# Cluster attention, then token mixing: argmax's equality in PSUM, masks on other engines, later mixing weights converted in the second half

## The chip, the cores and the metric

One core of a Trainium2 chip runs the kernel. The metric is the device time of one execution in microseconds; the median of several runs counts. The engines are TensorE (PE, with its weight loads PEld), VectorE (DVE), ScalarE (ACT), GpSimd (POOL) and SyncE (SP), whose queue issues most DMAs.

## The reference

For 4 batches and 8 heads of 768 tokens and width 64, each query and key is assigned to the nearest of 16 centroids, and a query sees only keys of its own cluster. The result, as rows of 512 channels, goes through a rotation by learned angles, a mixing over tokens with two 768 x 768 weights, and a channel mixing with a residual:

```python
q_assign = np.argmax(np.einsum('bhsd,hcd->bhsc', q_n, c_n), axis=-1)
k_assign = np.argmax(np.einsum('bhsd,hcd->bhsc', k_n, c_n), axis=-1)
mask = q_assign[:, :, :, None] == k_assign[:, :, None, :]
scores = np.where(mask, scale * np.matmul(q, k.transpose(0, 1, 3, 2)), -1000000000.0)
attn = np.exp(scores - np.max(scores, axis=-1, keepdims=True))
attn = attn / (np.sum(attn, axis=-1, keepdims=True) + 1e-09)
x = np.matmul(attn, v)            # as (batch, token, 512)
theta = x @ w_theta
y = np.einsum('ts,bsd->btd', w_tok_r, x * np.cos(theta))
y = y + np.einsum('ts,bsd->btd', w_tok_i, x * np.sin(theta))
u = x + y
return u + np.maximum(u @ w_ch, 0.0)
```

The weights w_theta, w_tok_r, w_tok_i and w_ch come as 64-bit floats. The kernel makes 32-bit floats of their bits itself, and splits every operand of its large products into a high and a low part.

## The kernel before, in words

**First half: attention.** The work goes by pairs of heads, 16 of them (4 per batch). Each pair has 12 units (two halves of the queries, six blocks of 128 keys). A loop takes two units at a time. In each turn PE makes score products for the current units (sc, line 374), score products for the maxima of units 10 ahead (m, also line 374), and the products of the exponentials with v (av, line 509). ScalarE takes the exponentials (line 437), VectorE the row maxima (nm, line 396), and GpSimd adds up exponentials (acc, line 448). Side work for later pairs is hung into the loop at fixed units by tables of numbers: A_UNITS for the assignment to clusters, W_UNITS and W_EVERY for the conversion of weights. Within the loop, each engine's instructions keep the order in which the code issues them; before and after it a scheduler orders them.

The assignment of a pair (assign, line 248) runs in steps. PE makes the logits of queries and keys against the centroids (lg) and transposes them into a tile of PSUM (lt). From the third pair on, lt takes its turn in a pool of two tiles (m_tile, line 196) with the score tiles of the maxima, so the second m tile after lt uses the same place. VectorE takes the maximum over the 16 centroids (mxl), compares (line 280), multiplies by falling weights so that the first of equal maxima wins (line 284), and takes the maximum (rr). The cluster numbers go through DRAM to 16 rows per head (clq, clk). From them come the two mask rows mq and mk, which add a huge negative number to a score product where the clusters differ (lines 330 to 340): mq by two ScalarE passes (for the second pair by GpSimd), mk by VectorE.

The row sums of a pair (sm, line 476) go through DRAM (sd), are turned to one over them on VectorE (sq, line 494), and come back (rb, line 499) for the normalisation (line 530).

**Weights.** to_f32 (line 118) loads a block of 64-bit weights, and makes 32-bit floats by one ScalarE pass (line 135) and four VectorE operations (lines 137, 140, 143, 146). split_w (line 150) makes the high part on ScalarE and the low part on GpSimd (line 159). During the attention half w_theta and the mixing weights of the first three token blocks are converted and kept in SBUF; those of the last three blocks (six pieces) are converted too and stored to DRAM as 32-bit floats (wd3r to wd5i, line 156).

**Second half: mixing.** For each batch and token block, theta (line 804) makes the angle product (tp, line 608), VectorE reduces the angle (kk, r, lines 613 to 615) and turns the block of x (xn, line 601), ScalarE takes sine and cosine, VectorE multiplies, and GpSimd makes the low parts (zlc, zls, line 830). mix (line 866) adds 48 products per block to y in PSUM. theta runs two blocks ahead of mix. After six blocks add_y (line 880) adds y to x on VectorE (line 887), and the channel products (line 899) follow. During the first batch, late (line 783) brings the remaining mixing weights from DRAM into u tiles (a ring of four), splits them on ScalarE and VectorE (lines 790 and 791), and converts w_ch in four chunks through the same ring; the channel's own operands use that ring next.

## Time and profile before

| | |
|---|---|
| median of 3 runs | 792.06 us (789.42 to 792.98) |
| the profiled execution | 792.87 us; its span 791.1 us |
| PE busy | 774.3 us |
| VectorE busy | 572.6 us |
| GpSimd busy | 488.3 us |
| ScalarE busy | 386.5 us |
| granted TensorE clock, mean | 0.991 |
| first product of the mixing | at 462.4 us |

How to read it: the profiled execution is one run, and its span reaches from the first to the last instruction. In rows of a timeline the first number is the start in us, the second the duration, then the engine and the line of the kernel, the operation, the tiles written and read, and in brackets how long the engine sat idle before it and what ended that. A busy PE is not PE at its peak.

### The profile page before, as it was taken

To read this page: it belongs to the slowest core of one execution; us is meant where nothing else is said; L and a number is where in the kernel's file an instruction comes from. 1 tells how busy PE (TensorE), PEld (TensorE's weight loads), DVE (VectorE), ACT (ScalarE), POOL (GpSimd) and SP (SyncE) were. 2 spreads that over 40 slices of the span, in tenths; PEclk is the share of its full clock that TensorE was granted. 3 is DMA by queue.
4 is the path that set the end of the run, shared out by engine and by line. 5 is a ranking of instruction groups with operands and counts; after the bars stand their busy time and mean duration, and the time that the engine had idled before them with its cause. 6 is when DMAs were issued, how large, how long until landed. Compare 5 with 4: busy or idle time off the path is not lost.

```text
span 791.1 us, 14306 instructions
## 1 busy us (share of the span) xinstructions
PE 774.3 (98%) x5538; PEld 572.9 (72%) x5538; DVE 572.6 (72%) x688; ACT 386.5 (49%) x777; POOL 488.3 (62%) x284
## 2 busy tenths in 40 slices
PE   6999999999999999999999799999999999999998
PEld 4656665666656565656665488899889988899998
DVE  5789999999999999999989659954445433634322
ACT  3366666767676676767556436341334123403310
POOL 3388789999999999888988432561215122332131
PEclk9899999999999999999999999999999999999999
DMA  3132324332433244324343467115011411030001
GB/s 120 61 98 72 93 95 151 93 123 91 151 104 125 81 149 151 119 84 164 112 161 109 101 182 206 24 31 173 15 27 28 160 27 27 14 94 15 1 21 61
DMA packets 81583, 73.43 MB, mean 93 GB/s; under 512 B 59588, under 2 KB 65324, under 8 KB 81132
## 3 DMA queue, kind: packets, MB, share of 16 engines
q1 hardware_dynamic: 81228, 72.10, 30.5%
q8 instruction: 43, 0.70, 0.4%
q10 hardware_dynamic: 288, 0.43, 0.1%
q14 instruction: 24, 0.20, 0.1%
HBM read 57.08 MB, written 15.32 MB: 92 GB/s over the span
## 4 chain that ended last, share of the span: by engine, by line
PE 91%; DVE 5%; DMA 2%; issue 1%; SPq 1%; ACT 1%; DVEq 0%
PE y L876 26%; PE sc L374 24%; PE av L509 15%; PE tp L608 8%; PE cy L899 5%; PE m L374 4%; PE cp L899 3%; PE sm L476 2%; PE lg L263 2%; PE y L899 1%; DVE acc L452 1%; PE lt L275 1%; DVE nm L396 1%; PE mt L404 1%; DVE xl L583 1%
## 5 line engine op out<-in xcount | busy, mean ns | idle before, releaser
L437 ACT ACTIVATE at<-sc 128x384 f32<-128x384 f32 x384 | 173.6, 493 | 96.0 <-PE m L374 50.5
L396 DVE TENSOR_REDUCE nm<-m 128x1 f32<-128x768 f32 x192 | 179.6, 945 | 21.4 <-PE m L374 18.3
L448 POOL TENSOR_TENSOR acc<-at,at 128x768 f32<-128x768 f32 x64 | 129.9, 2030 | 36.0 <-ACT at L437 36.0
L374 PE MATMUL m<-hk,hq 64*128 64x384 f32 x384 | 147.1, 387 | 0.9 <-DVE nm L396 0.8
L509 PE MATMUL av<-at,vt 128*64 128x384 f32 x768 | 145.7, 499 | 1.4 <-ACT at L437 1.2
L830 POOL TENSOR_TENSOR zlc<-ab,zhc 128x512 fp32r<-128x512 f32 x24 | 32.1, 1336 | 173.2 <-ACT zhc L828 173.2
L448 POOL TENSOR_TENSOR acc<-acc,at 128x768 f32<-128x768 f32 x64 | 132.4, 2068 | 10.1 <-ACT at L437 8.0
L374 PE MATMUL m<-mk,mq 64*128 64x384 f32 x384 | 127.7, 336 | 0.8 <-DVE mk L303 0.8
L374 PE MATMUL sc<-hq,hk 64*128 64x384 f32 x384 | 116.6, 388 | 0.5 <-ACT at L437 0.5
L374 PEld LDWEIGHTS sc<-hq,hk 64*128 64x128 f32 x384 | 55.8, 184 | 62.7 <-issue 27.9
L374 PE MATMUL sc<-mq,mk 64*128 64x384 f32 x384 | 97.6, 335 | 0.0
L374 PE MATMUL sc<-hq,lk 64*128 64x384 f32 x384 | 97.3, 334 | 0.0
L374 PE MATMUL sc<-lq,hk 64*128 64x384 f32 x384 | 97.3, 334 | 0.0
L509 PEld LDWEIGHTS av<-at,vt 128*64 128x64 f32 x768 | 46.7, 136 | 60.5 <-issue 53.6
L374 PEld LDWEIGHTS m<-hk,hq 64*128 64x128 f32 x384 | 70.7, 185 | 3.4 <-DVE nm L396 2.8
L374 PEld LDWEIGHTS m<-mk,mq 64*128 64x128 f32 x384 | 71.6, 188 | 1.1 <-ACT hq L356 1.1
L613 DVE TENSOR_SCALAR kk<-tp 128x512 int32<-128x512 f32 x24 | 16.4, 683 | 77.2 <-PE tp L608 77.2
L452 DVE TENSOR_TENSOR acc<-acc,acc 128x768 f32<-128x768 f32 x30 | 70.6, 2354 | 0.0
L581 ACT CAST xh<-xT 128x512 fp32r<-128x512 f32 x23 | 14.3, 622 | 99.7 <-PE tp L608 99.7
L890 POOL TENSOR_TENSOR ul<-xT,uh 128x384 fp32r<-128x384 f32 (+1 forms) x36 | 33.5, 957 | 35.4 <-ACT uh L889 34.9
L374 PEld LDWEIGHTS sc<-lq,hk 64*128 64x128 f32 x384 | 54.9, 186 | 0.0
L374 PEld LDWEIGHTS sc<-mq,mk 64*128 64x128 f32 x384 | 54.7, 184 | 0.0
(160 smaller groups left out, 1710.3 us busy)
## 6 DMA issues: line engine op xcount, KB each, us to landing
rawq<-in_qT_dram SPq DMA_DIRECT2D x16, 384.0 KB
vt<-in_v_dram SPq DMA_DIRECT2D x16, 384.0 KB
rb<-sd SPq DMA_DIRECT2D x32, 192.0 KB
xT_d<-xt SPq DMA_DIRECT2D x16, 384.0 KB
xb<-xT_d SPq DMA_DIRECT2D x96, 64.0 KB
rawk<-in_kT_dram SPq DMA_DIRECT2D x15, 384.0 KB
w<-in_wrT_dram SPq DMA_DIRECT2D x6, 768.0 KB
w<-in_wiT_dram SPq DMA_DIRECT2D x6, 768.0 KB
```

Source lines behind the costliest of these rows:

```text
L374: nc.tensor.matmul(out, lhsT=stat[r, cols], rhs=mov[r, over], start=start, stop=stop)
L396: nc.vector.tensor_reduce(out=s["nm", a][:, j, i // 2:i // 2 + 1], in_=s["m", j][:, :, 0:HS], op=ALU.max, axis=AX.XY, negate=True)
L437: last_exp[0] = nc.scalar.activation(out=s["at", a, i][:, j], in_=s["sc", j], func=AF.Exp, scale=SCALE)
L448: last_acc[0] = nc.gpsimd.tensor_tensor(out=s["acc", a, x], in0=prev, in1=at, op=ALU.add)
L452: nc.vector.tensor_tensor(out=s["acc", a, 0], in0=s["acc", a, 0], in1=s["acc", a, 1], op=ALU.add)
L509: nc.tensor.matmul(s["av"][64 * j:64 * j + 64], lhsT=s["vt"][:, i, j, :], rhs=s["at", a, i][:, j], start=(i == 0), stop=(i == NT - 1))
L608: nc.tensor.matmul(tp, lhsT=xx[:, c, :], rhs=w_th[c][k], start=(n == 0), stop=(n == 3 * NCT - 1))
L613: nc.vector.tensor_scalar_mul(kk, tp, INV_2PI)
L830: nc.gpsimd.tensor_tensor(out=zl, in0=tr, in1=zh.bitcast(F32), op=ALU.subtract)
L876: nc.tensor.matmul(y_at(b, d, c0, c1), lhsT=zz[:, d * P:(d + 1) * P], rhs=ww[:, c0:c1], start=first and lead, stop=last, skip_group_check= ...
L890: nc.gpsimd.tensor_tensor(out=ul[:, d, :], in0=x, in1=uh[:, d, :].bitcast(F32), op=ALU.subtract)
L899: nc.tensor.matmul(cp, lhsT=w_c[d][k][:, e * P:(e + 1) * P], rhs=uu[:, d, :], start=(n == 0), stop=(n == 3 * NCT - 1), skip_group_check=True)
```

## The change

It has four parts.

- The equality of the argmax writes back into lt in PSUM, as 32-bit floats, and the product with the weights reads it there, in the same step; the step after it keeps only the maximum rr.
- mk is made by one ScalarE pass (the absolute value of a scaled difference, with a scale and a bias per row), and mq, now minus one or zero, by one VectorE operation, for all pairs but the first. Four small constant columns and their writes replace one. The tables of units lose one step.
- The mixing weights of the last three token blocks are no longer converted in the attention half and no longer stored to DRAM. The ten conversions that stay are spread wider.
- late converts them from the 64-bit weights in the second half, in two chunks of 384 columns for each of the six pieces, with the low part on GpSimd.

```diff
-    ncl = cpool.tile([P, 1], F32, name="ncl")
-    nc.vector.tensor_scalar_mul(ncl, mcl, -1.0)
+    kscale = cpool.tile([P, 1], F32, name="kscale")
+    nc.vector.memset(kscale, 0.0)
+    kbias = cpool.tile([P, 1], F32, name="kbias")
+    nc.vector.memset(kbias, 0.0)
+    for r in (0, 64):
+        nc.vector.memset(kscale[r:r + C], BIG)
+        nc.vector.tensor_scalar_mul(kbias[r:r + C], mcl[r:r + C], -BIG)
+        nc.vector.memset(kbias[r + 32:r + 33], 1.0)
...
-    def split_w(hi, lo, src, cols, new, eng, most, kept=None):
+    def split_w(hi, lo, src, cols, new, eng, most):
...
-            if kept is not None:
-                nc.sync.dma_start(out=kept[:, sl], in_=w)
-                return
...
         nc.vector.tensor_tensor(
-            out=eq, in0=ltv, in1=mx.unsqueeze(2).broadcast_to([P, NG, C]), op=ALU.is_equal)
-        yield
-
-        nc.vector.tensor_tensor(out=eq, in0=eq, in1=wb, op=ALU.mult)
+            out=ltv, in0=ltv, in1=mx.unsqueeze(2).broadcast_to([P, NG, C]), op=ALU.is_equal)
+        nc.vector.tensor_tensor(out=eq, in0=ltv, in1=wb, op=ALU.mult)
+        yield
+
...
-        mq = st[pi]["mq"]
-        if pi == 1:
-
-            nc.gpsimd.tensor_scalar(out=mq, in0=cl["q"], scalar1=mcl, scalar2=None, op0=ALU.is_equal)
-        else:
-            nc.scalar.activation(out=mq, in_=cl["q"], func=AF.Abs, bias=ncl)
-            yield
-            nc.scalar.activation(out=mq, in_=mq, func=AF.Relu, scale=-1.0, bias=1.0)
+
+        nc.scalar.activation(out=st[pi]["mk"], in_=cl["k"], func=AF.Abs, scale=kscale, bias=kbias)
         yield
         nc.vector.tensor_scalar(
-            out=st[pi]["mk"], in0=cl["k"], scalar1=mcl, scalar2=mbi, op0=ALU.not_equal, op1=ALU.mult)
+            out=st[pi]["mq"], in0=cl["q"], scalar1=mcl, scalar2=-1.0, op0=ALU.is_equal, op1=ALU.mult)
...
-    A_UNITS = (-9, -4, -2, -1, 2, 2, 3, 6, 7, 7.9)
+    A_UNITS = (-9, -4, -2, -1, 2, 2, 3, 7, 7.9)
...
-        stages(W_FIRST if x == 0 else [W_EVERY * (x - 1) + k for k in W_UNITS], gen)
+        stages(W_FIRST if x == 0 else [NU * (3 * (x - 1) // 2) + k for k in W_UNITS], gen)
...
-            for w, x in ((w_r, "r"), (w_i, "i")):
-                hi, lo = w[t]
-                kept = u_tile("kept").rearrange("p c s -> p (c s)").bitcast(F32)[:, 0:S]
-                nc.sync.dma_start(out=kept, in_=w_d[t, x])
-                nc.scalar.copy(out=hi, in_=kept)
-                nc.vector.tensor_tensor(out=lo, in0=kept, in1=f(hi), op=ALU.subtract)
+            for w, src in ((w_r, wrT), (w_i, wiT)):
+                for gen in split_w(*w[t], src[t * P:(t + 1) * P], S, wt_pair, nc.gpsimd, CK):
+                    run(gen)
```

At three places the order of VectorE's instructions tells more than the diff. The numbers behind the names tell buffers apart, and lines are those of each kernel. The first place is the startup, from the squares of the centroids (csq) to their normalised copies (cnn); lq is the low part of the first pair's queries. Before:

```order
L216 TENSOR_TENSOR csq<-cin 128x64
L218 TENSOR_REDUCE cs<-csq 128x1
L360 TENSOR_TENSOR lq_162<-rawq_228,hq_161 128x768
L222 TENSOR_SCALAR cs<-cs 128x1
L223 RECIPROCAL cs<-cs 128x1
L226 TENSOR_SCALAR cnn<-cin,cs 128x64 x2
```

And now:

```order
L218 TENSOR_TENSOR csq<-cin 128x64
L356 TENSOR_TENSOR lq_164<-rawq_230,hq_163 128x768
L220 TENSOR_REDUCE cs<-csq 128x1
L224 TENSOR_SCALAR cs<-cs 128x1
L225 RECIPROCAL cs<-cs 128x1
L228 TENSOR_SCALAR cnn<-cin,cs 128x64 x2
```

The low part of the queries has moved ahead of the reduce.

The second place is the assignment of a later pair in the middle of the attention half, with the row maxima (nm) around it. Before:

```order
L278 TENSOR_REDUCE mxl_770<-lt_766 128x24
L280 TENSOR_TENSOR eq_772<-lt_766,mxl_770 128x384
L396 TENSOR_REDUCE nm_685<-m_0_775 128x1
L284 TENSOR_TENSOR eq_772<-eq_772,wc 128x384
L286 TENSOR_REDUCE rr_788<-eq_772 128x24
```

And now:

```order
L280 TENSOR_REDUCE mxl_771<-lt_767 128x24
L282 TENSOR_TENSOR lt_767<-lt_767,mxl_771 128x384
L284 TENSOR_TENSOR eq_773<-lt_767,wc 128x384
L392 TENSOR_REDUCE nm_686<-m_0_777 128x1
L288 TENSOR_REDUCE rr_789<-eq_773 128x24
```

The product has moved ahead of the row maximum, and it is the last reader of lt.

The third place is the end of the first batch in the second half, where y is added to x (xT). Before:

```order
L825 TENSOR_TENSOR r_0_6521<-r_0_6521,xn_0_6519 128x512
L601 STREAM_TRANSPOSE xn_2_6879<-xb_6643 128x512
L613 TENSOR_SCALAR kk_1_6620<-tp_1_6624 128x512
L583 TENSOR_TENSOR xl_3_6975<-xT_6515,xh_3_6974 128x512
L614 SCALAR_TENSOR_TENSOR r_1_6621<-kk_1_6620,tp_1_6624 128x512
L887 TENSOR_TENSOR xT_6021<-y_0_6154,xT_6021 128x384
```

And now, where wtmp is the u tile of a chunk of w_ch:

```order
L813 TENSOR_TENSOR r_0_6539<-r_0_6539,xn_0_6537 128x512
L143 TENSOR_SCALAR wtmp<-wtmp 128x512
L149 SCALAR_TENSOR_TENSOR wtmp<-wtmp 128x512
L593 STREAM_TRANSPOSE xn_2_6897<-xb_6661 128x512
L146 TENSOR_SCALAR wtmp<-wtmp 128x512
L152 SCALAR_TENSOR_TENSOR wtmp<-wtmp 128x512
L149 SCALAR_TENSOR_TENSOR wtmp<-wtmp 128x512
L605 TENSOR_SCALAR kk_1_6638<-tp_1_6642 128x512
L575 TENSOR_TENSOR xl_3_6993<-xT_6533,xh_3_6992 128x512
L152 SCALAR_TENSOR_TENSOR wtmp<-wtmp 128x512
L606 SCALAR_TENSOR_TENSOR r_1_6639<-kk_1_6638,tp_1_6642 128x512
L875 TENSOR_TENSOR xT_5955<-y_0_6116,xT_5955 128x384
```

The last conversions of w_ch have moved to just ahead of the first addition of y.

More of the change, by code (lines that the diff above doesn't have):

```diff
@@ L173 @@
     w_c = {}
-    w_d = {(t, x): dram.tile([P, S], F32, name=f"wd{t}{x}") for t in range(EARLY, NT) for x in "ri"}
     ma = [ctx.enter_context(tc.tile_pool(name="ma0", bufs=1))]
@@ L540, in early_weights @@
                 yield from split_w(*w[t], src[t * P:(t + 1) * P], S, raw_pair, nc.gpsimd, CKE)
-        for t in range(EARLY, NT):
-            for x, src in (("r", wrT), ("i", wiT)):
-                yield from split_w(
-                    None, None, src[t * P:(t + 1) * P], S, raw_pair, nc.gpsimd, CKE, kept=w_d[t, x])
     def run(gen):
```

3 lines of the change are left out of this document (1 added, 2 removed).

## The prediction

> **What bounds the kernel now.** I read the page first, then the stretches of the span, then the chain of waits around the end of the attention half, then single engines in time. The page and one stretch of the steady attention half (columns: stretch, its length, busy time of each engine, granted clock, DMA share, GB/s):
>
> ```profile
> PE 774.3 (98%) x5538; PEld 572.9 (72%) x5538; DVE 572.6 (72%) x688; ACT 386.5 (49%) x777; POOL 488.3 (62%) x284
> PE 91%; DVE 5%; DMA 2%; issue 1%; SPq 1%; ACT 1%; DVEq 0%
> 140.00:180.00 40.00, 40.00 (x332) 24.38 (x332) 37.82 (x37) 27.17 (x58) 39.38 (x19) 1.00 0.38 120
> ```
>
> PE is busy all 40 us there and has 91% of the chain. VectorE (37.82) and GpSimd (39.38) are nearly full beside it. So work taken off them in the steady half gains nothing by itself; the change pays or costs only where PE waits. The row sums of the softmax (L476) come once per pair of heads and serve as a clock:
>
> ```profile
> 67.47 0.85 PE L476 MATMUL sm<-acc,ecol 128*32 128x384 f32 x8
> 93.59 0.85 PE L476 MATMUL sm<-acc,ecol 128*32 128x384 f32 x8
> 120.08 0.85 PE L476 MATMUL sm<-acc,ecol 128*32 128x384 f32 x8
> 146.56 0.85 PE L476 MATMUL sm<-acc,ecol 128*32 128x384 f32 x8
> 172.51 0.85 PE L476 MATMUL sm<-acc,ecol 128*32 128x384 f32 x8
> ```
>
> The gaps are 26.12, 26.49, 26.48 and then 25.95, PE's own pace. Three early pairs lose 0.17, 0.54 and 0.53 us, 1.2 in all, to a VectorE that runs behind.
>
> **The change, part by part.** The sum goes by the profiled execution, 792.87 us (span 791.1 and 1.8 around it). The median of the three runs is 792.06, 0.8 below; I subtract that at the end.
>
> *Startup.* VectorE now does the split of the first q (lq) ahead of the reduce of the centroid squares. Before:
>
> ```profile
> 4.63 0.22 DVE L218 TENSOR_REDUCE cs<-csq 128x1 f32<-128x64 f32 x1
> 4.94 0.57 POOL L221 TENSOR_TENSOR cs<-cs,half 128x1 f32<-128x1 f32 x1 [2.51 <-DVE cs L218]
> 5.07 0.96 DVE L360 TENSOR_TENSOR lq<-rawq,hq 128x768 fp32r<-128x768 f32 x1 [0.21 <-ACT hq L356]
> 5.94 0.15 DVE L222 TENSOR_SCALAR cs<-cs 128x1 f32<-128x1 f32 x1
> 12.14 0.36 DVE L284 TENSOR_TENSOR eq<-eq,wc 128x384 bf16<-128x384 bf16 x1
> ```
>
> The square root on GpSimd ran under lq. Now the reduce starts at 6.03 (5.07 + 0.96), ends at 6.25, and after 0.09 of hand-over and 0.57 of GpSimd the next step starts at about 6.9, not 5.94: 0.95 us. PE's first logits wait for this. The product of equality and weight, 0.36 here from SBUF, becomes an operation on PSUM (0.56, next rows) on the same path: 0.2. Startup: +1.1. The added constants are ten small writes before the centroids have landed, at nothing; uncovered, at the 0.15 of the cs row, they would be 1.5 us.
>
> *Equality in PSUM.* A steady pair, VectorE and then PE's weight loads:
>
> ```profile
> 212.49 0.56 DVE L278 TENSOR_REDUCE mxl<-lt 128x24 f32<-128x384 f32 x1 [0.32 <-PE lt L275]
> 213.08 0.56 DVE L280 TENSOR_TENSOR eq<-lt,mxl 128x384 bf16<-128x384 f32 x1
> 213.55 0.95 DVE L396 TENSOR_REDUCE nm<-m 128x1 f32<-128x768 f32 x1
> 214.42 1.40 DVE L284 TENSOR_TENSOR eq<-eq,wc 128x384 bf16<-128x384 bf16 x1
> 214.01 0.18 PEld L374 LDWEIGHTS m<-hk,hq 64*128 64x128 f32 x1
> ```
>
> No operation of the trace writes PSUM from VectorE. The nearest rows, 0.56 for reading 384 columns of it, price both: the equality stays 0.56, and the product falls from 1.40 to 0.56. VectorE gains 0.84 a pair, and in the three early pairs that is more than the 0.54 lost at most: -1.2 (0 if the backlog refills). But lt sits in one of two m tiles, and the load at 214.01 begins the second score group after it, which writes that tile. Before, the tile was free at 213.64. Now it is free when the product ends: 213.64 + 0.03 + 0.56 = 214.23, and about 0.05 later for PE. PE stands in order, so score products queued behind this load wait too: 214.28 - 214.01 = 0.27 us. Thirteen pairs (3 to 15) place it so: +3.5. If both operations run 0.07 shorter it is 0.13 a pair (1.7); if 0.07 longer, 0.41 (5.3). I take the middle, which uses rows as they stand.
>
> The Trainium skill, page "SBUF — State Buffer", section "Who interferes with whom", says that VectorE and GpSimd share a port pair as an exclusive lock, and that a VectorE instruction with at most one SBUF input outside the two-port modes stays free of it. The trace agrees: the equality, one input in PSUM, took 0.56 beside a busy GpSimd, and the product, two in SBUF, 0.36 alone and 1.40 beside it.
>
> *Masks.* ScalarE drops one of two passes and VectorE does one operation of the old form at the old place. ScalarE is 27.17 of 40 busy; nothing follows. For the second pair the GpSimd mask goes, six units ahead of its use: nothing.
>
> *End of the attention half.* The conversions of the later weights leave. Columns: start, length, engine:
>
> ```profile
> 432.02 2.31 DVE L583 TENSOR_TENSOR xl<-xs,xh 128x512 fp32r<-128x512 f32 x1
> 434.25 2.58 DVE L146 SCALAR_TENSOR_TENSOR w<-w,w 128x768 int32<-128x768 int32 x1
> 436.87 0.32 SPq L156 DMA_DIRECT2D wd5i<-w  x1
> 437.28 0.38 SPq L492 DMA_DIRECT2D sq<-sd  x1
> 439.37 0.23 DVE L494 RECIPROCAL sq<-sq 128x12 f32<-128x12 f32 x1 [2.53 <-DMA sq<-sd]
> 439.51 0.63 DVE L613 TENSOR_SCALAR kk<-tp 128x512 int32<-128x512 f32 x1
> 437.47 1.07 PE L608 MATMUL tp<-wth_hi,xl 128*128 128x512 f32 x4
> 441.01 1.16 PE L608 MATMUL tp<-wth_hi,xh 128*128 128x512 f32 x4 [1.40 <-DVE r L614]
> ```
>
> SP's load of sq stood behind the store wd5i, which waited for L146; the reciprocal, kk, r and PE's next angle product stood behind that. Without the store, sq lands before kk can start. What is late next is kk's own input: PE ends it at 438.54, so kk starts 0.97 earlier than 439.51 and the rest moves with it: -1.0 (0 if sq is late for another reason). It cannot be more at this place, since xl waits for its inputs until about 432 anyway; PE's next waits belong to the rivals.
>
> *Second half.* Twelve chunks of 384 columns replace six loads and six subtracts (tile kept). Each needs four VectorE operations, and now also a GpSimd subtract. Stretch from the first mixing product to the sixth, whole and for kept alone (DVE, ACT); then VectorE's four steps on 512 columns with GpSimd idle, one of them beside a GpSimd subtract, and the size of such a subtract:
>
> ```profile
> 462.40:515.70 53.30, 53.30 (x290) 45.91 (x290) 42.70 (x58) 24.62 (x40) 18.47 (x13) 1.00 0.46 124
> 462.40:515.70 53.30, 7.62 (x6) 4.72 (x6) 1.00 0.46 124
> 490.12 0.41 DVE L137 TENSOR_SCALAR wtmp<-wtmp 128x512 f32<-128x512 f32 x1
> 490.57 0.43 DVE L140 TENSOR_SCALAR wtmp<-wtmp 128x512 int32<-128x512 int32 x1
> 491.03 0.69 DVE L143 SCALAR_TENSOR_TENSOR wtmp<-wtmp 128x512 int32<-128x512 int32 x1
> 491.98 0.68 DVE L146 SCALAR_TENSOR_TENSOR wtmp<-wtmp 128x512 int32<-128x512 int32 x1
> 494.12 1.53 DVE L137 TENSOR_SCALAR wtmp<-wtmp 128x512 f32<-128x512 f32 x1
> 493.77 1.60 POOL L159 TENSOR_TENSOR wch_lo<-wtmp,wch_hi 128x512 fp32r<-128x512 f32 x1 [7.65 <-ACT wch_hi L158]
> L890 POOL TENSOR_TENSOR ul<-xT,uh 128x384 fp32r<-128x384 f32 (+1 forms) x36 | 33.5, 957 | 35.4 <-ACT uh L889 34.9
> 519.04 0.74 DVE L887 TENSOR_TENSOR xT<-y,xT 128x384 f32<-128x384 f32 x2
> ```
>
> Four steps are 2.21 for 512 columns, 1.66 for 384, 19.9 for twelve chunks. Less 7.6 that go, 12.3 are added; VectorE is idle for 53.30 - 42.70 = 10.6. So even with every gap filled it is 1.7 late at the additions of y into x (519.04), which stand behind the last conversion of w_ch in its order, and on which PE's channel products wait. L137 beside GpSimd took 1.53, not 0.41: it waited out the subtract. Twelve subtracts of 0.96 are 11.5; if all fall on VectorE it is 13.2 late. The chunks pass through four u tiles, each loaded again only after the subtract of the chunk before: if for that reason no gap is filled, 23.8. The row beside GpSimd is nearest to what a stretch of conversions with their subtracts looks like, so I stay near 13.2 and take a little less, since PE reaches the channel some us after the first addition: +11.
>
> By the same page and section of the Trainium skill, whichever of the two engines starts first holds the pair for its whole instruction and the other blocks fully; it speaks against this part of the change. By it the term is 13.2, and without it 1.7.
>
> Sum: 792.9 + 1.1 - 1.2 + 3.5 - 1.0 + 11 = 806.3; less 0.8, **805.5 us**.
>
> **The rivals.**
>
> *The second half is hidden.* PE is busy in all 53.3 us there, and gaps fill at will. Then only 1.7 is late: 797.0 - 0.8 = 796.2. Against it: the order puts subtracts between conversions.
>
> *Nothing comes of it.* The m tile is free in time and the second half costs nothing: 792.9 + 1.1 - 1.2 - 1.0 - 0.8 = 791.0.
>
> *Faster: PE's waits at the end of the attention half go.*
>
> ```profile
> 449.18 1.24 PE L509 MATMUL av<-at,vt 128*64 128x384 f32 x4 [1.15 <-ACT at L437]
> 452.88 1.51 PE L476 MATMUL sm<-acc,ecol 128*32 128x384 f32 x8 [2.46 <-DVE xt L522]
> 455.59 2.08 PE L608 MATMUL tp<-wth_hi,xh 128*128 128x512 f32 x4
> 459.74 1.07 PE L608 MATMUL tp<-wth_lo,xh 128*128 128x512 f32 x4
> ```
>
> VectorE carries four operations like the 2.58 of L146 less here. If the waits of 1.40, 1.15 and 2.46 all go, 5.0 are won, and the first products afterwards are no longer slow (2.08 against 1.07 for four): 1.0. With 1.2 from the early pairs and none of the costs: 792.9 - 7.2 - 0.8 = 784.9. It decides if the chain there is load and not latency. Against it: after kk it runs through a table load, a sine and a copy, which do not change.
>
> *The ring of four tiles decides.* 23.8 late, and PE, idle for long, starts slowly again (1.0, as in the rows above): 806.3 - 11 + 24.8 - 0.8 = 819.3. For it: three generations of chunks follow each other; against it: the loads of a generation overlap its conversions.
>
> **How the numbers follow.** A measurement of this kernel tells about 0.5% (4.0 us: 788.1 to 796.0) from no change. Forecast 0.60, its own range 797 to 816 (second half 5 to 19, m tile 1.7 to 5.3, gains 1 to 2); hidden 0.15; nothing 0.05; faster 0.08; ring 0.12. Slower by over 0.5%: 0.60 + 0.12 + half of the hidden case, which lies on the bound: 0.79. Within: 0.05 and the other half: 0.13. Faster: 0.08. The range reaches from the nothing case to the top of the forecast: 790 to 817, and leaves out the faster case and the ring.
>
> **What would show it.** Right: the row sums 25.95 + 0.27 apart from the first gap on, with weight loads of m waiting for lt's product; PE's first logits about 1 us later; the sq reciprocal before kk; conversions of 384 columns that take 1 us and more beside GpSimd, the first xT additions 8 to 14 us later against the first mixing product, and PE idle ahead of the channel products of batch 0. The forecast is wrong if row sums stay 25.95 apart, or if PE passes from mixing to channel products in batch 0 without a wait; wrong in sign if the stretch from the last attention product to the first mixing product is shorter by 4 us or more.

## The result and the profile after

The changed kernel takes **816.57 us** (median of 4 runs, 814.48 to 817.79); beside it the kernel before took 792.52 us. The ratio is 1.0309 with a 95% interval of 1.0274 to 1.0344. The change makes the kernel about 3% slower. The profiled execution, the slowest of the four, is 817.79 us with a span of 816.0, 24.9 more than before.

Two lines of the page after, busy time and the chain that ended last, answer to the first two of before:

```profile
PE 783.9 (96%) x5538; PEld 577.7 (71%) x5538; DVE 550.0 (67%) x713; ACT 380.0 (47%) x776; POOL 486.9 (60%) x295
PE 80%; DVE 10%; DMA 4%; issue 2%; ACT 2%; POOL 1%; SPq 0%; DVEq 0%; ACTq 0%
```

VectorE's work fell by 22.6 us in the whole and its share of the chain rose from 5% to 10%: work left a place where it was hidden and came back in one where it is not. The places show by PE's own milestones, the first logits, then some row sums (the clock that the prediction used):

```profile
8.97 0.85 PE L265 MATMUL lg<-rawq,cb 128*32 128x384 f32 x1 [0.55 <-DVE cb L236]
69.87 0.85 PE L472 MATMUL sm<-acc,ecol 128*32 128x384 f32 x8
149.31 0.85 PE L472 MATMUL sm<-acc,ecol 128*32 128x384 f32 x8
176.06 0.85 PE L472 MATMUL sm<-acc,ecol 128*32 128x384 f32 x8
203.64 0.85 PE L472 MATMUL sm<-acc,ecol 128*32 128x384 f32 x8
229.94 0.85 PE L472 MATMUL sm<-acc,ecol 128*32 128x384 f32 x8
```

The first three gaps sum to 79.44 (before: 79.09), the next is 26.75, then one of 27.58, then 26.30, where before the fourth and those after it were 25.95. In the order of the program the 24.9 us are:

| from milestone to milestone | predicted | measured |
|---|---|---|
| start to first logits (7.88, now 8.97) | +0.95 | +1.1 |
| first logits to first row sum (67.47, now 69.87) | +0.2 | +1.3 |
| the next three gaps | -1.2, and part of the 3.5 | +0.4 |
| the ten gaps after them | the rest of the 3.5 | +5.3 |
| the last two gaps | -1.0 | -0.8 |
| last row sum to first mixing product | 0 | -1.0 |
| first mixing to first channel product | +11, with the next | +13.8 |
| first channel product to next angle product | | +4.8 |

(The 1.3 of the second row is not explained. The eight profiles with the changed kernel's code up to there, seven of them of experiments below, need 59.7 to 62.5 us from the first logits to the first row sum; the kernel before, masks, equality and the other five need 58.0 to 59.6. So equal code scatters by up to 2.8 us, but the two groups do not overlap, and neither masks nor equality alone shows the difference. The gap of 27.58 is this execution's own: the other seven have none above 26.8.)

**The steady pair.** VectorE's three operations on lt, then the score products on PE: the first score product of a group and the first product of the next m tile. Before, in order of time:

```profile
212.38 0.44 PE L374 MATMUL sc<-hq,hk 64*128 64x384 f32 x1
214.04 0.41 PE L374 MATMUL m<-hk,hq 64*128 64x384 f32 x1
```

and after:

```profile
270.32 0.56 DVE L280 TENSOR_REDUCE mxl<-lt 128x24 f32<-128x384 f32 x1 [0.39 <-PE lt L277]
270.91 0.57 DVE L282 TENSOR_TENSOR lt<-lt,mxl 128x384 f32<-128x384 f32 x1
271.51 0.56 DVE L284 TENSOR_TENSOR eq<-lt,wc 128x384 bf16<-128x384 f32 x1
270.21 0.44 PE L370 MATMUL sc<-hq,hk 64*128 64x384 f32 x1
272.18 0.18 PEld L370 LDWEIGHTS m<-hk,hq 64*128 64x128 f32 x1 [0.23 <-PE sc L370]
272.21 0.41 PE L370 MATMUL m<-hk,hq 64*128 64x384 f32 x1
```

The distance is 2.00, not 1.66. Writing PSUM cost 0.57, nearly what reading it did (0.56). The last reader of lt ends at 272.07, and the weight load of m begins 0.11 later. The row puts that load's wait down to PE's own score product; but in all 14 pairs from the third on, here and in the run equality below, the load comes 0.11 to 0.12 after the end of the product on VectorE, and before the change 0.37 to 0.46 after the end of the last reader.

**The end of the attention half.** The wait of 1.40 before the angle product is 0.52, and the first mixing product (before at 462.23, not at the 462.4 of the table) follows the row sums by 8.34 (before 9.35):

```profile
448.25 0.94 PE L600 MATMUL tp<-wth_hi,xh 128*128 128x512 f32 x3 [0.52 <-DVE r L606]
460.12 2.79 PE L472 MATMUL sm<-acc,ecol 128*32 128x384 f32 x16 [2.46 <-DVE xt L518]
468.46 0.51 PE L864 MATMUL y<-wr_hi,zhc 128*128 128x512 f32 x2
```

**The second half.** The stretch from the first mixing product to the first addition of y (xT), before and after (columns: stretch, length, then busy time of PE, PEld, DVE, ACT, POOL):

```profile
462.23:519.04 56.81, 56.81 (x311) 48.97 (x310) 46.18 (x63) 26.37 (x43) 21.01 (x15) 1.00 0.43 117
```

```profile
468.46:542.73 74.27, 62.40 (x338) 53.14 (x336) 64.68 (x102) 31.25 (x58) 34.67 (x26) 0.95 0.47 125
```

It is 17.46 longer. VectorE is busy for 18.50 more and idle for 9.59 (before 56.81 - 46.18 = 10.63): hardly any gap was filled. PE, busy to the end of that stretch before, is idle for 11.9 us of it. Its waits, the first addition, and the angle product that ends the channel:

```profile
524.26 0.62 PE L864 MATMUL y<-wi_hi,zhs 128*128 128x512 f32 x2 [1.30 <-ACT wi_hi L161]
525.71 0.62 PE L864 MATMUL y<-wi_lo,zhs 128*128 128x512 f32 x2 [0.83 <-POOL wi_lo L162]
543.93 1.01 PE L887 MATMUL cp<-uh,wch_hi 128*128 128x384 f32 x2 [10.94 <-ACT uh L877]
565.42 0.86 PE L600 MATMUL tp<-wth_hi,xh 128*128 128x512 f32 x3
542.73 0.74 DVE L875 TENSOR_TENSOR xT<-y,xT 128x384 f32<-128x384 f32 x2
```

The granted clock (the third figure from the end) was half until about 552:

```profile
536.00:538.00 2.00, 0.00 (x0) 0.50 0.00 0
548.00:550.00 2.00, 2.00 (x7) 2.00 (x7) 2.00 (x6) 2.00 (x5) 2.00 (x2) 0.50 0.00 0
552.00:554.00 2.00, 2.00 (x13) 2.00 (x12) 0.00 (x0) 0.00 (x0) 2.00 (x3) 0.95 0.53 83
```

The same step of a conversion on VectorE, once alone and once beside one of GpSimd's subtracts, then places where VectorE stood still, and where ScalarE did, although converted chunks were in the ring:

```profile
498.00 0.36 DVE L146 TENSOR_SCALAR wtmp<-wtmp 128x384 int32<-128x384 int32 x1
518.28 1.17 DVE L146 TENSOR_SCALAR wtmp<-wtmp 128x384 int32<-128x384 int32 x1
518.00 1.23 POOL L162 TENSOR_TENSOR wr_lo<-wtmp,wr_hi 128x384 fp32r<-128x384 f32 x1 [0.93 <-ACT wr_hi L161]
483.21 0.96 DVE L526 TENSOR_TENSOR xt<-xt,rb 128x768 f32<-128x768 f32 x1 [2.56 <-DMA rb<-sd]
491.69 0.71 DVE L593 STREAM_TRANSPOSE xn<-xb 128x512 f32<-128x512 f32 x1 [2.92 <-DMA xb<-xT_d]
497.61 0.36 DVE L143 TENSOR_SCALAR wtmp<-wtmp 128x384 f32<-128x384 f32 x1 [1.64 <-ACT wtmp L141]
```

```profile
490.42 0.93 ACT L161 CAST wr_hi<-wtmp 128x384 fp32r<-128x384 f32 x2 [1.53 <-DMA xT_d<-xt]
```

The first four chunks were converted by 477.5, but ScalarE's casts of them began at 490.42, after the last pair's attention (xt) had been stored; until then no u tile came free and no further chunk could be loaded. So nearly all of VectorE's idle time (third busy time) lies ahead of the second four chunks, and behind that point VectorE is full:

```profile
468.46:498.00 29.54, 29.54 (x164) 25.56 (x163) 20.56 (x35) 9.69 (x18) 11.55 (x9) 1.00 0.49 133
498.00:542.73 44.73, 32.86 (x176) 27.58 (x174) 44.12 (x67) 21.57 (x41) 23.13 (x17) 0.92 0.45 119
```

### The profile page after: what moved, and what is told of

It reads as the page before. It is cut to its first block, busy times and chain, and to the rows that moved or that the text cites. A ratio compares the mean times of both kernels' runs of the same rounds, so it can differ in the third digit from the quotient of the medians.

```text
span 816.0 us, 14363 instructions
## 1 busy us (share of the span) xinstructions
PE 783.9 (96%) x5538; PEld 577.7 (71%) x5538; DVE 550.0 (67%) x713; ACT 380.0 (47%) x776; POOL 486.9 (60%) x295
## 4 chain that ended last, share of the span: by engine, by line
PE 80%; DVE 10%; DMA 4%; issue 2%; ACT 2%; POOL 1%; SPq 0%; DVEq 0%; ACTq 0%
PE sc L370 23%; PE y L864 19%; PE av L505 15%; PE tp L600 6%; PE cy L887 5%; PE m L370 5%; PE cp L887 3%; DVE nm L392 2%; PE lg L265 1%; PE sm L472 1%; PE y L887 1%; DVE wtmp L149 1%; DVE acc L448 1%; PE lt L277 1%; DMA xT_d<-xt 1%
## 5 line engine op out<-in xcount | busy, mean ns | idle before, releaser
L444 POOL TENSOR_TENSOR acc<-at,at 128x768 f32<-128x768 f32 x64 | 124.0, 1937 | 60.1 <-ACT at L433 60.1
L444 POOL TENSOR_TENSOR acc<-acc,at 128x768 f32<-128x768 f32 x64 | 128.0, 2000 | 15.4 <-ACT at L433 13.5
L370 PE MATMUL sc<-lq,hk 64*128 64x384 f32 x384 | 99.5, 340 | 0.0
L370 PEld LDWEIGHTS sc<-hq,lk 64*128 64x128 f32 x384 | 55.0, 185 | 0.0
```

What stands on the lines that cost most here:

```text
L370: nc.tensor.matmul(out, lhsT=stat[r, cols], rhs=mov[r, over], start=start, stop=stop)
L444: last_acc[0] = nc.gpsimd.tensor_tensor(out=s["acc", a, x], in0=prev, in1=at, op=ALU.add)
```

## The experiments

**The three parts alone.** Each kernel is the one before with the lines of one part of the change and nothing else. Of each diff the telling lines are shown; a line of dots stands for lines left out, here and below.

```diff
...
-                nc.sync.dma_start(out=kept, in_=w_d[t, x])
...
+                for gen in split_w(*w[t], src[t * P:(t + 1) * P], S, wt_pair, nc.gpsimd, CK):
```

> The kernel before with the weights' part of the change alone (later mixing weights turned to f32 in the second half, early ones 18 units apart). Theory A, read from the trace of after: the chunks pass through the four u tiles one generation after the other, each waiting for the last one's subtract and for its own load, and PE then waits ahead of the channel products and restarts slowly: 13.8 us until the first channel product and 4.8 in the channel products, 18.6, less 1.9 at the end of the attention half: 792.5 + 16.7 = 809. Theory B, the prediction's: only VectorE's own work and its blocking by GpSimd count: +11 and -1.0: 802.5. Theory C, that the change's parts make each other worse (the equality in PSUM moves the end of the attention half): clearly under 802.

Measured: 806.33 us, ratio 1.0189 (1.0156 to 1.0222). From the first mixing to the first channel product 71.86 (before 61.70), with a wait of 10.00, then 20.52 (16.66) to the next angle product. The time lies between the two theories; the wait and the longer channel are Theory A's. This part carries most of the loss.

```diff
-            out=eq, in0=ltv, in1=mx.unsqueeze(2).broadcast_to([P, NG, C]), op=ALU.is_equal)
-        yield
-
-        nc.vector.tensor_tensor(out=eq, in0=eq, in1=wb, op=ALU.mult)
+            out=ltv, in0=ltv, in1=mx.unsqueeze(2).broadcast_to([P, NG, C]), op=ALU.is_equal)
+        nc.vector.tensor_tensor(out=eq, in0=ltv, in1=wb, op=ALU.mult)
+        yield
+
```

> The kernel before with the equality in PSUM alone. The prediction's price is 0.27 us for each of 13 pairs and 0.2 at the start, less 1.2 for the early pairs: 795.0. As the trace of after has it, row sums 26.31 apart and not 25.95: 13 x 0.36 = 4.7, 0.2 at the start and no gain for the early pairs: 797.4. Rival: the longer gaps of after come from the masks on VectorE or from the weights, and not from this part: row sums stay 25.95 apart, 792.7.

Measured: 795.10 us, ratio 1.0047 (1.0031 to 1.0063). The gaps are 26.39, 26.75, 26.75 and then 26.30: 0.35 a pair in the steady state, and no gain in the early pairs. That the time is the expected 795.0 is luck: the gaps of the profile add 3.9 us, as in the 797.4, and 1.9 came off ahead of the first row sum and behind the last one, where this part has nothing to win.

```diff
...
+        nc.scalar.activation(out=st[pi]["mk"], in_=cl["k"], func=AF.Abs, scale=kscale, bias=kbias)
...
-            out=st[pi]["mk"], in0=cl["k"], scalar1=mcl, scalar2=mbi, op0=ALU.not_equal, op1=ALU.mult)
+            out=st[pi]["mq"], in0=cl["q"], scalar1=mcl, scalar2=-1.0, op0=ALU.is_equal, op1=ALU.mult)
...
```

> The kernel before with the two masks on other engines alone. By the prediction: lq stands ahead of the reduce of the centroid squares, +0.95, and nothing in the pairs: 793.5, row sums 25.95 apart from the first steady gap on, first logits at about 8.9 us. Rival: the mask on VectorE is cheaper than the old one (0.83 us in the trace of after where before has 1.23), so that the three early gaps lose their 1.2 us: 792.3.

Measured: 795.95 us, ratio 1.0051 (1.0030 to 1.0071). The first logits come 0.93 later, as predicted, but there is more: two gaps of 27.30 and 27.28 among gaps of 25.95, and one of 26.16 instead of 24.52. Where such a gap begins, VectorE's last step of a conversion and GpSimd's low part of the keys (lk) start together. Before, VectorE got through:

```profile
228.94 0.94 DVE L146 SCALAR_TENSOR_TENSOR w<-w,w 128x768 int32<-128x768 int32 x1
228.94 2.63 POOL L360 TENSOR_TENSOR lk<-rawk,hk 128x768 fp32r<-128x768 f32 x1
```

With the masks moved, GpSimd starts 0.02 us ahead here and VectorE takes 1.70 us longer. The backlog runs on over the new mq, and ten us later PE waits for VectorE:

```profile
229.49 2.64 DVE L152 SCALAR_TENSOR_TENSOR w<-w,w 128x768 int32<-128x768 int32 x1
233.78 2.24 DVE L339 TENSOR_SCALAR mq<-clq,mcl 128x768 fp32r<-128x768 f32 x1
239.45 0.55 PE L281 MATMUL lt<-identf,lgs 128*128 128x128 f32 x3 [0.98 <-DVE nm L396]
```

```profile
229.47 1.85 POOL L360 TENSOR_TENSOR lk<-rawk,hk 128x768 fp32r<-128x768 f32 x1
```

In the kernel before VectorE wins all ten such meetings, in this one it loses three of ten (the three long gaps), in the changed kernel's profile one (its gap of 27.58), in seven later profiles with the same attention half none. The three ratios multiply to 1.0289, beside the whole change's 1.0309. That is near, but in part by chance, since the masks' ratio holds three lost meetings.

**tie: is it the meeting?** The masks' kernel, with GpSimd's lk one addition later.

```diff
-    LO_UNITS = dict(q=2, k=4)
+    LO_UNITS = dict(q=2, k=5.5)
```

> The kernel masks, with GpSimd's low part of k placed one addition later, so that it no longer starts at the same instant as VectorE's last conversion step. In the traces both start within 0.02 us of each other in every steady pair; in before VectorE comes first in 10 of 10 and takes 0.94, in masks GpSimd comes first in 3 of 10, the step takes 2.64, the mask behind it 2.24, and the row sum is 1.3 to 1.6 late. Theory T (the lost ties are the price of the masks): no gap over 26 in the steady pairs and 793.0, the start alone. Rival: the step meets another long GpSimd operation in the new order: gaps of 26.3 and more in several pairs, 795 and above.

Measured: 793.60 us (10 runs), ratio 1.0033 (1.0017 to 1.0049). All steady gaps are 26.00 to 26.02. lk now meets no conversion step:

```profile
231.93 1.82 POOL L360 TENSOR_TENSOR lk<-rawk,hk 128x768 fp32r<-128x768 f32 x1
```

So the meetings were the cause of the long gaps. (The time alone would not show it: the intervals of the two ratios overlap.) What is left of the masks' loss is mostly the startup and 0.05 a pair.

**late5: a small dose.** The kernel before, with only the last token block's weights (four chunks) converted late.

```diff
-        for t in range(EARLY, NT):
+        for t in range(EARLY, NT - 1):
...
+                if t == NT - 1:
+                    src = wrT if x == "r" else wiT
+                    for gen in split_w(hi, lo, src[t * P:(t + 1) * P], S, wt_pair, nc.gpsimd, CK):
+                        run(gen)
+                    continue
```

> The kernel before, but the last row of mixing weights alone (four of the twelve chunks) is turned to f32 in the second half. Theory A: a single generation has no chunk ahead of it to wait for, and VectorE has 10.6 us of gaps, so the second half costs nothing, and the attention half ends 1.0 to 1.9 us earlier because the store of the last converted row is gone: 790.6 to 791.5. Theory B (load): four chunks are 6.6 us less the two subtracts' 2.5, and four GpSimd subtracts 3.8, together under the 10.6 of gaps: the same. Rival: the gaps do not fill at all, +4.1 to +7.9 with the gain of 1.9: 794.7 to 798.5.

Measured: 796.97 us, ratio 1.0072 (1.0048 to 1.0096). This is within the rival's 794.7 to 798.5: the gaps did not fill. The first addition comes 62.48 after the first mixing product (before 56.81), with VectorE busy for 4.4 more and idle for 1.2 more. PE reaches the channel only 2.0 later, but the channel then takes 21.06, not 16.66. PE's two waits, and its clock (last but two) in two stretches:

```profile
523.40 0.62 PE L904 MATMUL cp<-uh,wch_hi 128*128 128x384 f32 x2 [1.82 <-ACT uh L894]
526.00 0.69 PE L904 MATMUL cy<-uh,wch_hi 128*128 128x384 f32 x1 [1.06 <-ACT uh L894]
```

```profile
524.00:525.00 1.00, 0.87 (x3) 0.66 0.40 62
530.00:531.00 1.00, 1.00 (x4) 0.50 0.72 112
```

A third of the chunks brings 5.67 of the 17.46 us at the first addition. Of that 3.69 goes into the slack that the channel products had, so only 2.0 of the 13.8 us arrive there; but in the channel it is already 4.4 of the 4.8: that price comes with the first small wait.

**warm and late5w: is it the clock?** Idle products ahead of the first channel products, 110 in the changed kernel, 40 in late5. The lines are late5w's.

```diff
+                for _ in range(NWARM if (b, ch, e) == (0, 0, 0) else 0):
+                    with tc.issue_after(last_mix[0].ins):
+                        nc.tensor.matmul(cp[:, 0:P], lhsT=identb, rhs=identb, start=True, stop=True)
```

(In warm they write a bank of their own.)

> The kernel after, with 110 idle products of 128 columns on PE between the last mixing product of batch 0 and the first channel product, so that PE is not idle while it waits there. Theory A: of the 4.8 us that the channel products of batch 0 take longer (21.49 against 16.66), most is the clock, which stands at 0.50 for about 8 us after the wait: 816.6 - 3.4 to 4.8 = 811.8 to 813.2. Rival: the additions of y to x come in late one by one and PE waits for each of them, so the clock costs nothing: 816.6.

Measured: 818.53 us, ratio 1.0332 (1.0310 to 1.0355). The 110 products were through 4.60 us before the first channel product and the clock fell after them; the order of the channel's products had moved too, and PE waited 3.08 and 1.23 more. The channel took 24.45. So the run did not do what it was built for, and the time fits neither theory.

> The kernel late5, with 40 idle products of 128 columns (1.84 us) on PE between the last mixing product of batch 0 and the first channel product. In late5 PE waited 1.82 and 1.06 us there, its clock then stood at 0.50 for about 6.3 us, and the channel products took 21.06 us against 16.66. Theory C (the clock is the price): with PE kept busy the clock stays at 1.00, 3.2 us come back: 793.8. Rival (the additions of y to x come in one by one and PE would wait for them at full clock too): 796 to 797.

Measured: 800.18 us, ratio 1.0119 (1.0090 to 1.0149), beyond both theories. The 40 products took 2.41 us, again the order of the channel's products moved, the waits were 1.27, 2.56 and 1.17, and the clock fell to 0.50. (Two of its row sums' gaps are 27.28: meetings as in masks can be lost without any edit of the masks.) Neither run parts the clock from the other reading, that the additions come one at a time and PE only follows them.

The traces of other runs bound the two. In the changed kernel these are the last three of the eight casts uh that the channel products of batch 0 read, and the product that waits for the seventh (by the order of PE's waits for ScalarE):

```profile
549.34 1.44 ACT L877 CAST uh<-xT 128x384 fp32r<-128x384 f32 x3
552.94 0.33 PE L887 MATMUL cp<-uh,wch_hi 128*128 128x384 f32 x1
```

The seventh cast ends at 550.32 and the clock is back at 552.20, so with a full clock that product, and all behind it, could have come at most 2.6 us earlier; in late5 the same working gives 2.8. The rest of the 4.8 (and of the 4.4), 2.2 (1.6) or more, is additions and casts that come late. That the clock has a price of its own is shown by split, splitact and splitvec below, where all eight casts were done 2.84 us after the first channel product and PE did not wait again: their channels began with 4.27, 3.75 and 5.44 us at half the clock and took 18.69, 18.47 and 19.24 us, 2.03, 1.81 and 2.58 over the 16.66.

**recip: the chain through the last reciprocal.** The changed kernel, with VectorE's first four late chunks held behind the reciprocal of the last row sums.

```diff
+        with tc.issue_after(hold[0].ins) if hold[0] is not None else nullcontext():
...
-        nc.vector.reciprocal(out=sq, in_=sq)
+        last_recip[0] = nc.vector.reciprocal(out=sq, in_=sq)
...
+            hold[0] = last_recip[0] if t == EARLY else None
```

> The kernel after, with VectorE's part of the first four chunks held back until the reciprocal of the last row sums is done. Theory A (a serial chain): the casts of the first chunks wait for the last store of the attention half, which hangs on that reciprocal; it was issued at 474.33 behind conversions and its input was there about 4.5 us earlier, so everything behind moves up: 816.6 - 4.5 = 812.1. Theory B (VectorE's total work sets the end): the same work in another order, 816.6.

Measured: 813.03 us, ratio 1.0270 (1.0247 to 1.0293), near Theory A. ScalarE's first casts came at 485.58, 5.1 earlier against the first mixing product, the first addition 2.9 earlier. The chain is part of the loss, the smaller one.

**split: is it the ring of four?** The changed kernel, the chunks in rings of their own in the same memory, three tiles for raw bits and six for floats.

```diff
...
-        t = u_tile("wtmp").rearrange("p c s -> p (c s)").bitcast(F32)
-        return t[:, 0:2 * CK], t[:, 2 * CK:3 * CK]
+        return (mt.tile([P, 2 * CK], F32, tag="wraw", name="wraw", bufs=3),
+                mt.tile([P, CK], F32, tag="ww", name="ww", bufs=6))
```

> The kernel after, with the late chunks in two rings of their own in the same memory (three raw tiles, free after the last conversion step, and six f32 tiles, free after the low part) in place of four tiles that hold both; the u tiles take that memory over afterwards. Theory A (the ring): loads of a later generation no longer wait for casts and subtracts of the one before; VectorE was idle for 9.6 us while conversions were outstanding, so 7 to 10 come back: 806.6 to 809.6. Theory B (VectorE's work and the blocking by GpSimd): 0 to 2: 814.6 to 816.6.

Measured: 820.85 us, ratio 1.0374 (1.0352 to 1.0395). The first addition came 75.49 after the first mixing product (74.27 in the changed kernel). So more room for chunks brought nothing, as Theory B has it, though the time is beyond both. The channel's first cast then waited for the rings' memory, PE for 12.95, which is a price of this edit.

**lowvec and actlow: GpSimd's subtracts.** The changed kernel with the late chunks' low parts on VectorE, and with a ScalarE copy in their place.

```diff
-                for gen in split_w(*w[t], src[t * P:(t + 1) * P], S, wt_pair, nc.gpsimd, CK):
+                for gen in split_w(*w[t], src[t * P:(t + 1) * P], S, wt_pair, nc.vector, CK):
```

> The kernel after, with the low parts of the twelve late chunks on VectorE and not on GpSimd. Theory B (the blocking by GpSimd is what costs): the conversions lose what they waited, about 6 us, and 12 subtracts of about 0.56 come on, 6.7: 815.5 to 817.5, and conversion steps stay at 0.35 and 0.55. Theory A (the ring): a tile is free about 0.6 us earlier in each of three generations, but stands in VectorE's order: 814.5 to 818. The time alone does not tell them apart; the lengths of the conversion steps and the order of the loads do.

Measured: 813.37 us, ratio 1.0274 (1.0252 to 1.0295). The stretch to the first addition:

```profile
466.59:532.52 65.93, 62.13 (x338) 53.13 (x336) 59.89 (x108) 30.44 (x56) 22.31 (x13) 1.00 0.52 140
```

It is 8.3 shorter than in the changed kernel, although VectorE does twelve operations more: 4.8 less busy and 3.5 less idle. But part of that is work moved: four of the sixteen conversion steps of w_ch now stand between the additions, and the channel took 25.87. From the first mixing product to the angle product behind the channel it is 4.0 shorter (93.0 against 97.0). The time is below both theories.

Actlow has instead:

```diff
-            eng.tensor_tensor(out=lo[:, sl], in0=w, in1=hi[:, sl].bitcast(F32), op=ALU.subtract)
+            if eng is None:
+                nc.scalar.copy(out=lo[:, sl], in_=w)
+            else:
+                eng.tensor_tensor(out=lo[:, sl], in0=w, in1=hi[:, sl].bitcast(F32), op=ALU.subtract)
...
-                for gen in split_w(*w[t], src[t * P:(t + 1) * P], S, wt_pair, nc.gpsimd, CK):
+                for gen in split_w(*w[t], src[t * P:(t + 1) * P], S, wt_pair, None, CK):
```

> The kernel after, with the low parts of the twelve late chunks left out: ScalarE writes a copy of the f32 weights in their place, so GpSimd has no subtract of a late chunk and VectorE none either (the output is that of other weights). Theory B (VectorE's own work and what GpSimd blocks of it): the stretch of the conversion steps falls as in lowvec, from 9.6 to about 4 us, and lowvec's 6.2 us of subtracts on VectorE are gone too: the first channel product stands 61 to 63 us after the first mixing product (75.5 in after, 67.1 in lowvec, 61.7 in before), 801 to 806. Theory A (loads that wait generation by generation): a tile is still free only after casts, the first casts still wait for the last store, and it stays at 66 to 68: 810 to 813.

Measured: 810.43 us, ratio 1.0237 (1.0202 to 1.0273). The first channel product stands 70.87 after the first mixing product, later than both theories have it. No step of w_ch has moved behind the first addition here, so this is the plain price of the subtracts: the stretch is 4.6 shorter, 3.5 of it busy time, and to the angle product behind the channel it is 4.2:

```profile
465.65:535.32 69.67, 61.85 (x338) 53.11 (x336) 61.16 (x103) 38.03 (x73) 24.22 (x15) 0.98 0.51 135
```

**splitact and splitvec: both at once.** Split rings together with each of these edits, in case the subtracts hide what the ring costs (the lines are splitvec's).

```diff
...
+        return (mt.tile([P, 2 * CK], F32, tag="wraw", name="wraw", bufs=3),
...
-                for gen in split_w(*w[t], src[t * P:(t + 1) * P], S, wt_pair, nc.gpsimd, CK):
+                for gen in split_w(*w[t], src[t * P:(t + 1) * P], S, wt_pair, nc.vector, CK):
```

> The kernel after with both edits: two rings of their own for the late chunks (split) and ScalarE's copy in place of the twelve low parts (actlow; the output is that of other weights). If the two causes hide each other, nothing is left but VectorE's own steps, 15.7 us more and 5.3 less in about 11 us of gaps: the first channel product stands 61 to 65 us after the first mixing product (70.9 in actlow, 83.2 in split), 799 to 804. If neither is the cause, it stays at 69 or more: 808 and above.

> The kernel after with two rings (split) and the twelve low parts on VectorE (lowvec). If the two causes hide each other: VectorE's steps and 6.2 us of subtracts, against lowvec's 67.1 from the first mixing to the first channel product: 63 to 66, 807 to 811. If the ring does not matter once GpSimd is out: 67 as in lowvec, 812 to 814.

Measured: splitact 814.80 us, ratio 1.0280 (1.0245 to 1.0316), first addition 67.64 after the first mixing product (actlow 69.67); splitvec 819.87 us, ratio 1.0337 (1.0296 to 1.0379), first addition 65.08 after (lowvec 65.93). Both times are spoilt by the cast's wait for the rings' memory (12.12 and 17.19 on PE). Room in the ring moves the first addition by 2.0, 0.9 or, with the subtracts on GpSimd, -1.2, and part of the first two is again work moved: in splitact four and in splitvec nine of the sixteen steps of w_ch stand behind the first addition. It does not decide.

**best: what is left without the change.** The kernel before, with none of the change. The store that stood ahead of the sq load (wd5i) comes 3.5 units later, and 50 idle products fill PE's wait of 2.46 before the last row sums.

```diff
+        if pi == NPAIR - 1:
+            warm = bank("warm")
+            for _ in range(50):
+                nc.tensor.matmul(warm[:, 0:P], lhsT=identb, rhs=identb, start=True, stop=True)
...
-        stages(W_FIRST if x == 0 else [W_EVERY * (x - 1) + k for k in W_UNITS], gen)
+        last = x == NCT + 2 * NT - 1
+        stages(W_FIRST if x == 0 else [W_EVERY * (x - 1) + k + 3.5 * (last and k == W_UNITS[-1]) for k in W_UNITS], gen)
```

> The kernel before with none of the change, but its last store of converted weights issued 3.5 units later, behind the load of the row sums, and 50 idle products of 128 columns on PE ahead of the last row sums, where PE waits 2.46 us. Theory: the wait of 1.40 ahead of the angle products goes (0.9 won, as in late5) and the clock does not fall to 0.50 behind the wait (1.0 won): 792.0 - 1.9 = 790.1. Rival: PE's clock falls in the waits of 1.15 before and in spite of it, and only 0.9 is won: 791.1; or the products delay the row sums: 792.

Measured: 789.94 us (12 runs), ratio 0.9981 (0.9967 to 0.9996), faster than both kernels by little. The wait of 2.46 is filled, the clock stays at 1.00 through the stretch in which it was 0.50 before, and the first mixing product comes 391.55 after the first row sum (before 394.76, 462.23 - 67.47):

```profile
448.78 2.97 PE L475 MATMUL warm<-identb 128*128 128x128 bf16 x50
452.00:458.00 6.00, 6.00 (x37) 1.00 0.95 324
```

```profile
452.00:458.00 6.00, 5.12 (x22) 0.50 0.95 312
```

(The first fence is best, the second the kernel before.) The wait of 1.40 is 0.52 here too, but the last two gaps of the row sums shorten by only 0.43 (by 0.83 in the changed kernel). The larger part is the clock, and the products only make sure of it: of the 23 executions of the kernel before that were measured beside best, eight have best's mean clock of 0.996 as well, and they take 789.21 to 790.29 us. So the weights' part is not needed for such a gain at the end of the attention half, which is small either way.

## Why the prediction was right or wrong

**The sign and the cause were right, the size was half.** It foresaw 13.4 us more of the profiled time, by PE's wait for the late conversions above all; 24.9 came. The 816.57 lies just above the forecast's own range (797 to 816; the ends that it names add up to 797.9 and 816.5).

**The second half: the step that failed most.** The prediction put the first addition 13.2 late, and it came 17.46 late. Actlow, which has the conversions without the subtracts, takes the sum apart (VectorE's busy time to the first addition: before 46.18, actlow 61.16, changed kernel 64.68):

| term | predicted | measured |
|---|---|---|
| added steps of VectorE | 12.3 | 15.0 (61.16 - 46.18) |
| waiting for GpSimd's subtracts | 11.5 | 3.5 (64.68 - 61.16) |
| gaps filled | -10.6 | -1.0 (9.59 - 10.63) |
| first addition late by | 13.2 | 17.5 |

What failed is "gaps filled": VectorE was idle for 9.59 as before, and 9.0 of it lies ahead of 498. There it waits for rb, xb and the next four chunks, and the four in the ring were already converted, so there was nothing to fill the gaps with. The subtracts were priced three times too high, the steps too low (46 of the 48 take 24.2 us in actlow, where 19.1 was priced). These errors of 9.6, 8.0 and 2.7 offset each other for the most part, so that 13.2 came near 17.46 owes much to luck. Recip shows that the chain through the last reciprocal is worth 2.9 of the lateness; how the rest of the idle time divides among the chains was not settled.

The Trainium skill, page "SBUF — State Buffer", section "Who interferes with whom", says that the engine that starts second is blocked for the other's whole instruction. Single meetings bear it out: the step at 518.28, 0.28 behind a subtract, took 1.17 and not 0.36. Taken as a sum over all twelve subtracts it was too much: 3.5 of 11.5.

**The channel: a term that was missing.** Before, the first addition was 4.89 ahead of the first channel product; of the 17.46, this slack took 3.69, where the prediction took 2.2 off (13.2 to 11), and 13.8 was left. Nothing was priced in the forecast for what follows when the slack is gone (the ring's rival had 1.0): the channel took 4.8 more, at most 2.6 of it by the clock and the rest by additions that come late one by one. With that the second half is 18.6 where 11 stood.

**Rivals.** Hidden, nothing and faster are out. The ring's 819.3 is the nearest number to 816.57, and its gaps did stay unfilled; but split, splitact and splitvec speak against its mechanism: room in the ring moves the first addition by 2.0 at most.

**Equality.** The mechanism is the one foretold: the m tile's next use waits for the product on PSUM. The size was 0.35 a pair, not 0.27, for the most part since the weight load went on 0.12 after the product and not 0.05.

**Early pairs.** The 1.2 that VectorE's lighter load was to give back did not come (equality: 26.39, 26.75, 26.75). Those pairs did not lose time to the multiply that went. The traces point to the conversions that stand there, whose steps GpSimd holds up. Before, in the second gap:

```profile
97.58 1.84 POOL L360 TENSOR_TENSOR lk<-rawk,hk 128x768 fp32r<-128x768 f32 x1
97.84 2.12 DVE L146 SCALAR_TENSOR_TENSOR w<-w,w 128x512 int32<-128x512 int32 x1
```

In weights and in the changed kernel, where the conversions are spread wider, the third early gap has no such step and is 25.95 (26.32), between two of 26.5 (26.8). But the first gap has one too and loses less, and no run took such a step away alone; what holds these pairs is not shown.

**Masks: "nothing" was wrong.** The start was foretold at 0.95 and measured at 0.93 (the constants, two columns with eight writes, not four with ten, cost nothing there). But the moved operations shift VectorE and GpSimd by hundredths of a us, and a conversion step is held up by lk. Masks pays 4.0 in all; tie takes 2.35 off (1.4 by the ratios). In the changed kernel's profile one meeting was lost, 1.27.

**End of the attention half.** The reasoning held: without the store sq was in time, and the last gap shortened by 0.88 (1.0 foretold). The further 1.0 after the row sums is not the change's. The first mixing product follows the last row sums by 9.3 to 9.5 us in before, masks, weights and late5, whose clock is at 0.50 for 6.83 us around there; by 8.3 to 8.4 in the changed kernel, equality, tie and others, where that lasts 3.41; and by 6.6 and 6.8 in best and actlow, where the clock does not fall. Equality and tie have none of the weights' part, so this differs from one execution to the next.

## What to carry to other kernels

A gap in an engine's time counts as room only if the operands of the work to be moved are there when it opens; find what each gap waits for before subtracting it. When a consumer had slack, price separately what uses it up and what its own restart costs afterwards, since the first small wait here cost as much as the long one. When a sum comes near, look at its terms: here three wrong ones offset each other. And look for two engines that hold each other up and start within a few hundredths of a us of each other: any edit elsewhere can turn the order.

## What was not expected of the hardware

In late5 the granted clock fell about 0.9 us after a single wait of 1.82 us of PE (0.66 in the mean of 524 to 525) and came back only near 531, though PE was busy for all of 526 to 531. In the traces the stretches at 0.50 behind PE's waits last 3.41, 6.83, 10.24, 13.65, 17.07 or 20.48 us, whole multiples of 3.41. The Trainium skill, page "TensorE: Matmul & The Clock Gate", section "What's actually happening", names an idle window of about 3.4 us; here 1.82 us of idle time in a single wait was enough.

A meeting of two engines within 0.02 us goes one way ten times in ten in one kernel and turns in three of ten in another. Who is recorded first does not tell who wins: in masks VectorE's start is recorded 0.02 behind in the three that it loses and 0.005 to 0.013 behind in the seven that it wins, and in late5w it loses two at 0.005. Each lost one costs VectorE 1.70 us, and 1.3 to 1.6 of it shows in the gap of the row sums (27.28 for 25.95, 26.16 for 24.52).
